# Sixteen small products ahead of TensorE's first work in a fused attention and gated MLP kernel

## The chip, the cores and the metric

The kernel runs on one core of a Trainium2 chip. The metric is the device time of one execution in microseconds; lower is better. Times of a kernel are medians over several runs.

## The reference

All inputs are float32. Chunked attention over 4 x 8 heads of 768 positions with 64 values each: a chunk of 32 queries sees 8 memory positions and a window of up to 56 positions around it. What it gives, 512 wide per position, goes through a gated MLP: a product with `w_in` and a rectifier, a split into u and v, a normalization of v, a product of v along the sequence with `w_spatial`, the gate, and a product with `w_out`.

```python
scores = scale * np.matmul(q_c, k_full.transpose(0, 1, 3, 2))
scores = scores - np.max(scores, axis=-1, keepdims=True)
a = np.exp(scores)
a = a / (np.sum(a, axis=-1, keepdims=True) + 1e-09)
out[:, :, c_start:c_end] = np.matmul(a, v_full)
...
h = np.maximum(x @ w_in, 0.0)
u, v = (h[..., :d_ff // 2], h[..., d_ff // 2:])
mu = np.mean(v, axis=-1, keepdims=True)
var = np.mean((v - mu) ** 2, axis=-1, keepdims=True)
v_n = (v - mu) / np.sqrt(var + 1e-06)
v_s = np.einsum('ts,bsd->btd', w_spatial, v_n) + b_spatial[None, :, None]
gated = u * v_s
return (gated @ w_out).astype(np.float32)
```

## The kernel before

Attention goes in 24 units of 128 queries (four chunks, all heads), six units to a batch element. A unit is one step of `attend`: `burst` (line 600) issues the scores of unit i, and the products of weights and values of unit i - 1, as short runs of small float32 products, 32 for each part. The profile shows two matmuls with a weight load each for one such product, so a part is 64 matmuls, 128 instructions; from unit 4 on both parts stand in one burst of 256 instructions. `softmax` (from line 700) has VectorE take the maximum and the difference (lines 713, 717) and ScalarE the exponential (line 732). `flip` turns p and the attention output: for the first nine units on TensorE (lines 788 and 815, tiles pt and xt), later on VectorE. Everything behind that is products in pairs of high and low parts (float32r), issued in `group` (line 872): three products for each pair of operands, from 384 to 512 columns wide. Weights are split into such pairs by `from_f64` (lines 1056 to 1084) as their loads land; `stage_w` and `stage_z` are the tiles for half of `w_in`.

All of this goes into a list of operations (`Plan`). `Plan.order` lays them out in time by given costs and writes one fixed order per engine; `ORDER` shifts single operations. The order of TensorE's instructions is therefore the same in each run, and each engine takes its own in that order. The planner also counts TensorE's instructions and lets a page of `PAGE` = 256 of them be fetched while the one before it runs (lines 205 to 210); that count begins at its first operation.

Ahead of the plan (lines 329 to 338) GpSimd writes `ident`, a unit matrix of 128 x 128, VectorE fills small constants, and ScalarE makes `minus` from `ident`. TensorE does nothing there. PSUM has eight banks' worth of tiles: four "f", and pools for "sx" (scores), "pt" and "xt".

Of the kernel before, what the change touches and what calls it, by code (L numbers as in the profile page):

```python
# [8 lines left out]
F32 = mybir.dt.float32  # L9
# [9 lines left out]
CH = 32  # L19
# [40 lines left out]
}  # L60
PAGE = 256
FETCH = 2.4
VLATE = 0
PSUB = 0
# [41 lines left out]
class Plan:  # L106
# [42 lines left out]
    def order(self):  # L149
# [19 lines left out]
        while len(out) < len(ops):  # L169
# [31 lines left out]
            if count:  # L201
# [3 lines left out]
                for m in range(begun, begun + count):  # L205
                    if m % PAGE == 0:
                        at = max(at, fetched.get(m // PAGE, 0.0))
                        fetched[m // PAGE + 1] = max(at, pipe) + FETCH
                    at += each
# [34 lines left out]
def tile_chunked_attention_gmlp(  # L244
# [22 lines left out]
    nc = tc.nc  # L267
    B, H, D, S = q.shape
# [4 lines left out]
    P = 128  # L273
# [29 lines left out]
    def pool(name, **kw):  # L303
        return ctx.enter_context(tc.tile_pool(name=name, **kw))
# [12 lines left out]
    ps = {name: pool(f"ps_{name}", bufs=sizes[name], space=PSUM) for name in ("f", "sx", "pt", "xt")}  # L317
# [7 lines left out]
    ident = const.tile([P, P], F32, name="ident")  # L325
# [3 lines left out]
    halves = const.tile([P, 2], F32, name="halves")  # L329
    warm = const.tile([P, 1], F32, name="warm")  # L330
    make_identity(nc, ident)
    nc.vector.memset(mhalf, -0.5)
    nc.vector.memset(tiny, 1e-9)
    for r in range(2):
# [1 line left out]
        nc.vector.memset(halves[r * D:(r + 1) * D, r:r + 1], 1.0)  # L336
    nc.scalar.activation(warm, mhalf, AF.Exp)
    nc.scalar.activation(minus, ident, AF.Copy, scale=-1.0)

    hot = [n for n in HOT]  # L340

# [875 lines left out]
```

## Time and profile before

| | |
|---|---|
| median of 3 runs | 383.62 us (383.19 to 385.25) |
| span of the profiled execution | 383.0 us |
| its TensorE matmuls | 358.4 us busy (94%) |
| ScalarE, VectorE, GpSimd | 253.2 (66%), 205.2 (54%), 152.3 us (40%) |

The span runs from the first to the last instruction of one profiled execution. A matmul row and its weight load are two instructions; sums over "PE" are matmuls alone, "PEld" the weight loads. "Idle before <- X" is time in which the engine did nothing and what ended it; "issue" means that the profile shows nothing that ended it. Semaphore instructions are not in these rows. Queue 8 and queue 14 carry instructions, queue 1 the loads and stores that SyncE issues; the share of a queue is the time of its packets over the time of 16 DMA engines in the stretch, put down to the stretch in which a packet starts (so it can be above the stretch itself).

### The profile page before, as it was taken

What the parts mean: (1) busy time and instruction counts of PE and PEld (TensorE: products, weight loads), DVE (VectorE), ACT (ScalarE), POOL (GpSimd) and SP (SyncE); (2) the same over time, 40 slices, a digit from 0 to 9 for tenths busy, and PEclk for the clock granted to TensorE, in tenths of its full rate; (3) what the DMA queues carried; (4) which work ended last, traced back from release to release, by engine and by line L of the source; (5) the groups of instructions that cost most, each with busy time, mean ns of one, the idle gap of its engine ahead of it and who ended that gap; (6) DMA issues with size and microseconds to landing.
All of it is one profiled execution on the core that took longest, in us unless ns stands there. A gap on an engine that the chain in (4) does not pass through costs nothing.

```text
span 383.0 us, 11256 instructions
## 1 busy us (share of the span) xinstructions
PE 358.4 (94%) x4692; PEld 321.0 (84%) x4692; DVE 205.2 (54%) x408; ACT 253.2 (66%) x659; POOL 152.3 (40%) x230
## 2 busy tenths in 40 slices
PE   1484999989999999999999999999999999999996
PEld 0353898989899889899899889899899889999995
DVE  1785877866436366665546274764555363613030
ACT  5873998863575968878876878879777883411212
POOL 5781887556424323325614423304514410213031
PEclk9998799999999999999999999999999999999999
DMA  7988926862123154124121433115120100000202
GB/s 225 319 272 183 317 84 154 288 192 82 34 86 105 72 146 98 50 75 146 48 86 55 170 90 107 50 49 171 51 86 2 55 29 2 1 0 3 82 0 84
DMA packets 29243, 39.71 MB, mean 104 GB/s; under 512 B 5192, under 2 KB 23304, under 8 KB 29192
## 3 DMA queue, kind: packets, MB, share of 16 engines
q1 hardware_dynamic: 28968, 38.91, 32.6%
q8 instruction: 37, 0.61, 0.7%
q14 instruction: 14, 0.11, 0.1%
q10 hardware_dynamic: 224, 0.08, 0.1%
HBM read 32.69 MB, written 6.29 MB: 102 GB/s over the span
## 4 chain that ended last, share of the span: by engine, by line
PE 81%; ACT 7%; DVE 4%; issue 3%; POOL 2%; DMA 1%; SPq 0%; ACTq 0%; POOLq 0%
PE f L872 70%; PE sx L602 8%; ACT xs L690 2%; POOL st L1058 2%; ACT pT L363 2%; PE pt L788 1%; DMA big<-in_moe_w_in_dram 1%; PE xt L815 1%; DVE mx L713 1%; ACT p L732 1%; PE f L602 1%; DVE p L717 1%; ACT big L991 1%; DVE vn L934 0%; ACT pT L791 0%
## 5 line engine op out<-in xcount | busy, mean ns | idle before, releaser
L872 PE MATMUL f<-wsp_h,vn 128*128 128x384 f32 x384 | 99.1, 339 | 0.0
L872 PE MATMUL f<-x,win_h 128*128 128x384 f32 x256 | 72.6, 341 | 0.0
L872 PEld LDWEIGHTS f<-wsp_h,vn 128*128 128x128 f32 x384 | 69.3, 188 | 2.6
L872 PE MATMUL f<-wout,big 128*128 128x512 f32 (+1 forms) x300 | 71.4, 382 | 0.0
L872 PE MATMUL f<-wsp_l,vn 128*128 128x384 f32 x192 | 64.5, 336 | 0.0
L690 ACT COPY xs<-sx 32x128 f32<-32x128 f32 x240 | 61.4, 256 | 3.5 <-PE sx L602 0.6
L872 PE MATMUL f<-win_h,x 128*128 128x512 f32 x192 | 62.9, 408 | 0.5 <-ACT x L821 0.2
L872 PEld LDWEIGHTS f<-wout,big 128*128 128x128 f32 x300 | 54.3, 188 | 9.1
L988 POOL TENSOR_TENSOR st<-st,u 128x384 f32<-128x384 f32 x32 | 33.4, 1044 | 66.9 <-DVE st L984 45.9
L872 PEld LDWEIGHTS f<-x,win_h 128*128 128x128 f32 x256 | 47.0, 188 | 1.4
L915 POOL TENSOR_TENSOR rstd<-ve,mhalf 128x1 f32<-128x1 f32 x24 | 15.3, 637 | 74.1 <-DVE ve L911 65.0
L363 ACT COPY pT<-p 32x128 f32<-32x128 f32 x144 | 42.6, 296 | 2.3 <-POOL p L768 0.5
L872 PE MATMUL f<-x,win_l 128*128 128x384 f32 x128 | 43.3, 338 | 0.0
L872 PEld LDWEIGHTS f<-win_h,x 128*128 128x128 f32 x192 | 35.2, 191 | 7.7 <-DVE x L825 0.5
L991 ACT CAST big<-st 128x384 fp32r<-128x384 f32 x32 | 16.4, 512 | 35.8 <-POOL st L988 35.4
L984 DVE TENSOR_TENSOR st<-f,bias 128x384 f32<-128x384 f32 x32 | 17.8, 556 | 39.4 <-PE f L872 39.0
L872 PE MATMUL f<-win_l,x 128*128 128x512 f32 x96 | 38.3, 399 | 0.3 <-DVE win_l L1084 0.3
L872 PEld LDWEIGHTS f<-wsp_l,vn 128*128 128x128 f32 x192 | 36.1, 188 | 0.0
L995 DVE TENSOR_TENSOR big<-st,big 128x384 fp32r<-128x384 f32 x32 | 19.4, 606 | 24.8 <-ACT big L991 24.8
L768 POOL TENSOR_TENSOR p<-p,rec 128x512 f32<-128x512 f32 x15 | 15.7, 1046 | 40.8 <-DVE rec L745 39.9
L363 POOL COPY pT<-p 32x128 f32<-32x128 f32 x96 | 29.9, 312 | 4.3
L602 PEld LDWEIGHTS sx<-k,q 64*32 64x32 f32 x1536 | 17.8, 112 | 14.2 <-POOL k L363 7.7
(91 smaller groups left out, 514.4 us busy)
## 6 DMA issues: line engine op xcount, KB each, us to landing
out_dram<-st SPq DMA_DIRECT2D x23, 256.0 KB
k<-in_k_dram SPq DMA_DIRECT2D x7, 800.0 KB
q<-in_q_dram SPq DMA_DIRECT2D x7, 768.0 KB
vmain<-in_v_dram SPq DMA_DIRECT2D x38, 128.0 KB
vmain<-in_v_dram SPq DMA_DIRECT2D x37, 96.0 KB
big<-in_moe_w_spatial_dram SPq DMA_DIRECT2D x6, 384.0 KB
big<-in_moe_w_in_dram SPq DMA_DIRECT2D x4, 512.0 KB
stage_w<-in_moe_w_in_dram SPq DMA_DIRECT2D x4, 512.0 KB
```

Source lines behind the costliest of these rows:

```text
L363: (nc.scalar.copy if e == "ACT" else nc.gpsimd.tensor_copy)(o, a)
L602: nc.tensor.matmul(o, w_, m, start=start, stop=True, skip_group_check=True)
L690: (nc.scalar.copy if e == "ACT" else nc.vector.tensor_copy)(o, a)
L713: nc.vector.tensor_reduce(mx, s, axis=AX.X, op=ALU.max)
L768: (nc.vector if e == "DVE" else nc.gpsimd).tensor_tensor(p3, p3, rec, op=ALU.mult)
L872: nc.tensor.matmul(o, ll if x == 1 else lh, rl if x == 2 else rh, start=x == j == 0, stop=j == len(pairs) - 1 and x == (single[-1] if sing ...
L915: nc.gpsimd.tensor_tensor(a, t_["ve", i], mhalf, op=ALU.pow)
L984: nc.vector.tensor_tensor(alloc("st", s_, [P, HT], F32), t_["f", n], bias[:, tok], op=ALU.add)
L988: nc.gpsimd.tensor_tensor(a, a, t_["u", i], op=ALU.mult)
L991: nc.scalar.copy(t_["g", i][:, 0, 0:HT], t_["st", s_])
L995: nc.vector.tensor_tensor(a[:, 1, 0:HT], t_["st", s_], a[:, 0, 0:HT].bitcast(F32), op=ALU.subtract)
L1058: nc.gpsimd.tensor_scalar(o, a, 2.0 ** -112, None, op0=ALU.mult)
```

## The change

Behind the constants, and ahead of the first operation of the plan, TensorE gets sixteen float32 products of `ident` with itself: 64 rows, 32 columns of weights, two moving columns each. They write two columns of a PSUM tile of tag "xt", which nothing reads. The plan, its order and all other instructions stay as they are. In TensorE's stream each instruction behind them stands 64 places further on.

```diff
--- before.py
+++ after.py
@@ -59,6 +59,7 @@
     319: (31, 0, ''), 320: (-34, 3, ''), 321: (-34, 1.5, ''), 323: (-32, 0.4, ''),
 }
 PAGE = 256
+PADS = 16
 FETCH = 2.4
 VLATE = 0
 PSUB = 0
@@ -329,6 +330,7 @@
     halves = const.tile([P, 2], F32, name="halves")
     warm = const.tile([P, 1], F32, name="warm")
     make_identity(nc, ident)
+    ps_pad = ps["xt"].tile([P, 512], F32, tag="xt", name="xt")
     nc.vector.memset(mhalf, -0.5)
     nc.vector.memset(tiny, 1e-9)
     for r in range(2):
@@ -336,6 +338,9 @@
         nc.vector.memset(halves[r * D:(r + 1) * D, r:r + 1], 1.0)
     nc.scalar.activation(warm, mhalf, AF.Exp)
     nc.scalar.activation(minus, ident, AF.Copy, scale=-1.0)
+
+    for _ in range(PADS):
+        nc.tensor.matmul(ps_pad[0:CH, 0:2], ident[0:D, 0:CH], ident[0:D, 0:2], start=True, stop=True)
 
     hot = [n for n in HOT]
```

## Rows read from the trace of the kernel before

**Rows 1.** The page: span, TensorE's busy time with instructions, and its instruction queue.

```profile
span 383.0 us, 11256 instructions
...
PE 358.4 (94%) x4692; PEld 321.0 (84%) x4692; DVE 205.2 (54%) x408; ACT 253.2 (66%) x659; POOL 152.3 (40%) x230
...
q8 instruction: 37, 0.61, 0.7%
```

**Rows 2.** Waits of TensorE: waiter, releaser: us in total, times, longest us.

```profile
PE f L602 <- issue: 5.3, 1, 5.3
...
PE xt L815 <- DVE xs L665: 1.1, 1, 1.1
```

**Rows 3.** Timeline, TensorE: start us, us, line, tile, shapes, count [idle before, releaser].

```profile
5.49 1.19 PE L602 MATMUL sx<-k,q 64*32 64x64 f32 x64 [5.49 <-POOL k L363]
...
22.58 0.86 PE L602 MATMUL f<-vmain,pT 64*32 64x64 f32 x64
...
26.13 0.50 PE L872 MATMUL f<-win_h,x 128*128 128x512 f32 x1 [0.24 <-ACT x L821]
...
31.87 0.78 PE L602 MATMUL f<-vmain,pT 64*32 64x64 f32 x49
37.93 0.46 PE L602 MATMUL f<-vmain,pT 64*32 64x64 f32 x15 [5.29 <-issue]
```

**Rows 4.** Stretches: us, then PE, PEld, DVE, ACT, POOL busy, clock, DMA, GB/s.

```profile
0.00:32.60 32.60, 17.83 (x474) 12.89 (x475) 18.57 (x40) 20.52 (x34) 20.14 (x27) 1.00 0.85 269
...
0.00:166.40 166.40, 145.15 (x2337) 126.21 (x2337) 104.11 (x212) 118.92 (x271) 88.30 (x114) 0.98 0.51 156
0.00:193.70 193.70, 172.45 (x2719) 151.51 (x2719) 120.17 (x239) 140.16 (x334) 100.34 (x138) 0.98 0.49 148
...
38.30:42.80 4.50, 4.50 (x107) 3.75 (x108) 3.38 (x5) 3.72 (x6) 3.73 (x3) 0.50 0.87 290
...
82.37:383.00 300.63, 297.31 (x3382) 270.35 (x3382) 148.78 (x293) 191.95 (x553) 98.49 (x175) 1.00 0.22 71
```

**Rows 5.** DMA queues (packets, MB, share) in 20.8:20.95, 21:35.25 and 35.25:35.45 us.

```profile
q8 instruction: 1, 0.02, 45.7%
...
q1 hardware_dynamic: 1691, 3.36, 87.0%
...
q8 instruction: 1, 0.02, 35.5%
```

**Rows 6.** Timeline, GpSimd, first 6 us.

```profile
1.06 0.29 POOL masks.py:199 TENSOR_SCALAR_AFFINE_SELECT ident<-ident 128x128 f32<-128x128 f32 x1
```

**Rows 7.** Timeline, SyncE's loads around 26 us.

```profile
25.75 0.81 SPq L385 DMA_DIRECT2D stage_w<-in_moe_w_in_dram  x2
```

**Rows 8.** Timeline, ScalarE, then VectorE, 33 to 37 us.

```profile
33.24 0.66 ACT L1056 ACTIVATE stage_z<-stage_w 128x512 f32<-128x512 f32 x1 [4.77 <-DMA stage_w<-in_moe_w_in_dram]
...
36.51 0.61 ACT L732 ACTIVATE p<-p 128x512 f32<-128x512 f32 x1
...
33.93 0.43 DVE L1066 TENSOR_SCALAR stage_z<-stage_z 128x512 uint32<-128x512 uint32 x1 [3.39 <-ACT stage_z L1056]
```

**Rows 9.** Timeline, TensorE, around two later bursts.

```profile
166.43 0.86 PE L602 MATMUL sx<-k,q 64*32 64x64 f32 x64
...
169.37 0.34 PE L872 MATMUL f<-x,win_l 128*128 128x384 f32 x1
...
193.72 0.86 PE L602 MATMUL sx<-k,q 64*32 64x64 f32 x64
...
196.31 0.33 PE L872 MATMUL f<-wsp_l,vn 128*128 128x384 f32 x1
```

**Rows 10.** DMA queues in 167.4:167.55, 193.2:194.9 and 194.9:195.05 us.

```profile
q8 instruction: 1, 0.02, 40.2%
...
q1 hardware_dynamic: 286, 0.52, 80.6%
...
q8 instruction: 1, 0.02, 44.8%
```

## The prediction

> **What bounds the kernel now.** I read the page first. TensorE is busy 94% of the 383.0 us, and 37 packets of queue 8 carry 0.61 MB of instructions for 9384 recorded matmuls and weight loads [rows 1]: 16.4 KB and some 254 of these per packet. With the semaphore instructions between them that is 256 instructions of 64 bytes, the size the kernel calls PAGE. So TensorE's stream is fetched in pages of 256, and 37 x 256 - 9384 = 88 instructions are semaphores, one per 107 others.
>
> Next the waits of TensorE. One wait has no releaser, 5.3 us before a matmul of line 602 [rows 2]. The timeline puts it inside a burst: 49 matmuls run from 31.87 us, nothing follows for 5.29 us, and the other 15 start at 37.93 [rows 3]. A burst needs nothing between its 49th and 50th matmul, so I take this as a page that was not there. Up to there 474 matmuls have run [rows 4], 948 matmul instructions, so the border lies just behind them and the other borders are 256 instructions apart from it. The DMA view agrees: queue 8 has no packet from 21.0 to 35.25 us, then one starts that takes 35.5% x 16 x 0.2 = 1.14 us [rows 5]. It ends by about 36.5, and TensorE goes on 1.47 us later. From the packet's start to the restart it is 2.6 us.
>
> From 82.37 us on TensorE is busy 297.31 of 300.63 us [rows 4]: any stall there goes straight to the end. Before it, TensorE also waits for the other engines; the last such wait is 1.1 us for VectorE's xs [rows 2].
>
> **The products themselves.** Sixteen float32 products are 64 instructions, 32 matmuls with their loads: a burst of 32 products is 64 matmuls [rows 3]. By the nearest row, the burst at 5.49 (64 matmuls in 1.19 us), they cost 0.6 us [rows 3]. They need ident, whose select on GpSimd starts at 1.06 and takes 0.29 us [rows 6], so they run at about 1.4 to 2.0. TensorE is idle until 5.49 and waits there for GpSimd's k [rows 3]; that wait hides them with 3.4 us to spare. Cost 0; if the cover were gone, 0.6 us. They write the bank of xt, which no other work uses so early, and put nothing on another queue. A gain is excluded for the products alone, since nothing waits for them.
>
> **The border that stalls.** Each border moves 64 instructions (32 matmuls) back. The one at the 50th matmul of the burst at 31.87 goes to its 18th. What it fetches is needed a page later; the page that was late is the one that begins at this border, and its request went out at the border before, one page earlier: 128 matmuls back from the stall, less a few semaphores, at the matmul of 26.13 [rows 3]. From there to the packet it is 9 us. At 25.75 SyncE had issued two loads of 512 KB [rows 7], and between 21.0 and 35.25 the load queue kept 87% of the engines' time [rows 5]: the fetch stood behind loads. Moved by 32 matmuls the request goes out inside the burst at 22.58, near 22.9 [rows 3], before those two loads are issued. The page is needed at 32.0, so its packet may start as late as 32.0 - 2.6 = 29.4, 6.5 us after the request. A fetch did get in at 20.8, in traffic as full as this [rows 5]; I expect this one by about 28, when the loads issued ahead of it are through (an estimate between 22.9 and 29.4), and the 5.29 us go.
>
> The Trainium skill says of a DMA engine's queues (DMA: Bandwidth & Descriptors, Queues, rings and completion order) that an engine takes turns between queue rows, packet by packet. By that rule no fetch would wait 9 us behind loads; the rows disagree, and I go by them.
>
> **What is late next.** Not much is won by it. The work behind the burst is the turning of p, and p is written by ScalarE's exponential at 36.51, which ends at 37.12 [rows 8]. Its chain has nothing of TensorE in it: ScalarE waited 4.77 us for a load of stage_w until 33.24, VectorE behind it until 33.93, with the maximum and difference of p queued behind that [rows 8]. So TensorE reaches the turning at 37.12 in place of about 37.93 + 0.40: a gain of 1.2 us, not 5.3. The moved fetch also takes 1.14 us of one DMA engine ahead of stage_w in place of behind it; where that engine is the last to land, the chain starts later by as much and 0.1 us is left. Above, the clock: it is 0.50 from 38.3 to 42.8, 4.50 us of work [rows 4]. TensorE had idled since 32.65; in the new order it idles from about 33.1 to 37.1, so I expect the lower level (1.2 GHz) again. Were it at 2.4 GHz, 2.25 us more would go, 3.4 us in all. Between 0.1 and 3.4 I take 0.7 us, near the row of p, and expect the chain to xs at 82.37 to follow, since its engines too are fed by TensorE in that stretch.
>
> **The borders that become tight.** Behind 82 us the bursts are 128 matmuls, 256 instructions: exactly a page, in 1.5 us. A border early in a burst asks for the page that is needed just behind the burst. To 166.40 us 2337 matmuls have run [rows 4]: (2337 - 474) x 2 = 3726 instructions behind the stall, with one semaphore per 107 some 3761; the 15th border behind the stall (3840) lies 79 instructions into the burst that starts at 166.43 [rows 9]. The fetch row confirms it: a packet starts in 167.4 to 167.55 [rows 10], 1.0 us into the burst. Moved by 64, the border lies 15 instructions in, and the next one 15 instructions (7.5 matmuls) behind the burst's end, reached at 169.2 [rows 9]. 64 instructions of the burst take 0.35 us, so the packet starts near 167.1, takes 40.2% x 16 x 0.15 = 0.97 us [rows 10], and with the 1.47 us of the stall the page is there at 169.6: a stall of 0.4 us. The burst at 193.72 is the same (2719 matmuls [rows 4], border 76 in, 12 after the move). Its fetch starts in 194.9 to 195.05, right behind output stores that fill 193.2 to 194.9 [rows 10]. An earlier request doesn't get past them: 194.95 + 1.08 + 1.47 = 197.5, needed at 196.3 [rows 9]: 1.2 us; without the stores 0.9. A third burst of this kind, at 221.7, comes out near zero by the same reckoning. Bounds: the 1.47 us rest on one stall. Were the page usable as soon as its packet ends, all these stalls would be 0; two or three more borders that come right ahead of a burst could add up to 1 us, so 0 to 2.6. I take 1.5.
>
> **The sum.** The span of 383.0 stands 0.6 below the median of 383.62, and I carry that over: 383.0 - 0.7 + 1.5 + 0.6 = 384.4.
>
> **Rivals.** (a) *The gain carries through and the new borders hold*: the early gain is 1.2 to 3.4 us and no page is late. For it: fetches already overlap all but one border; against it: three bursts of 1.5 us with a turnaround of at least 2 us. 383.6 - 2.3 = 381.3, range 380.2 to 382.4. (b) *The new borders cost more than the old one*: slower. Its place is the code right behind the bursts at 166, 194 and 222; it decides once packet start to restart exceeds the 2.5 us used there. With the one that needed 2.6 plus 1 us of queueing behind stores or loads, each of the three loses about 1 us more: 383.6 - 0.5 + 3.9 = 387.0, range 385.5 to 388. (c) *The idle is no page border*, or the moved request meets the same traffic: the 5.29 us stay, the late borders count or not: 383.6 to 385.1, say 384.0. The Trainium skill's rule (Runtime: NRT & Kernel Launch, Instruction fetch mechanics) that crossing a 16 KiB boundary is mostly hidden would make the whole change worth nothing, 383.6; the 5.29 us in mid-burst speak against it.
>
> **How the numbers follow.** Forecast 0.52; (a) 0.18; (b) 0.18; (c) 0.12. A 0.5% step is 1.9 us, about what a measurement of this kernel can tell from no change: below 381.7 it is faster, above 385.5 slower. Of (a) about two thirds are below 381.7; of (b) all, and a few per cent of the forecast, are above 385.5. Faster 0.13, same 0.66, slower 0.21. The forecast's own bounds are 383.6 - 1.2 + 0 = 382.4 to 383.6 - 0.1 + 2.6 = 386.1; the range of 382.0 to 386.3 leaves out most of (a) and half of (b).
>
> **What would show it.** Right: no idle with no releaser at 32 to 38 us, TensorE waiting instead for ScalarE's p at about 37.1, a queue 8 packet between 23 and 28, and short idles with no releaser some 2.7 us behind the starts of the bursts near 166 and 194. Wrong: the turning of p much earlier than 37, which means that its chain isn't bound by stage_w; the clock at full level in 38 to 43; or a queue 8 packet that still waits for 35. If the late bursts show no idle, the 1.47 us of the one stall were not the fetch's own and the time falls to about 382.9.

## The result, and the profile after

The changed kernel took 387.99 us (median of 15 runs, 384.78 to 389.79), the kernel before, run beside it, 384.38. The ratio is 1.0083, with an interval of 1.0059 to 1.0108: slower by about 0.8%. The forecast was 384.4 in a range of 382.0 to 386.3; the time lies above it, in the range of rival (b), but not for that rival's reason. Two later measurements of the same code gave 1.0102 (1.0049 to 1.0155) and 1.0056 (1.0026 to 1.0085). A ratio leaves out runs that took over 1.5% more than the fastest run of the same kernel.

The profiled execution of the changed kernel took 389.5 us. The page shows TensorE as busy as before [rows 1] in a span 4.3 us longer:

```profile
span 387.3 us, 11320 instructions
...
PE 363.5 (94%) x4724; PEld 325.0 (84%) x4724; DVE 204.1 (53%) x408; ACT 253.8 (66%) x659; POOL 150.5 (39%) x230
...
q8 instruction: 37, 0.61, 0.7%
```

TensorE's waits with no releaser and its wait for xs, from the view of waits (waiter, releaser: us in total, times, longest):

```profile
PE sx L607 <- issue: 3.8, 2, 2.6
PE xt L820 <- DVE xs L670: 2.6, 2, 2.3
PE f L607 <- issue: 2.6, 1, 2.6
```

Where there was one wait with no releaser, of 5.3 us [rows 2], there are three. The timeline of TensorE places them (the first line is that of the sixteen products):

```profile
1.41 1.86 PE L343 MATMUL xt<-ident 64*32 64x2 f32 x32 [1.41 <-POOL ident masks.py:199]
...
19.10 0.43 PE L607 MATMUL sx<-k,q 64*32 64x64 f32 x7 [2.62 <-issue]
...
28.10 0.64 PE L607 MATMUL f<-vmain,pT 64*32 64x64 f32 x20 [2.58 <-issue]
...
37.66 1.02 PE L607 MATMUL f<-vmain,pT 64*32 64x64 f32 x64
39.39 0.66 PE L793 MATMUL pt<-ident,p 128*128 128x128 f32 x4 [0.71 <-ACT p L737]
...
41.51 0.86 PE L607 MATMUL sx<-k,q 64*32 64x64 f32 x64
...
59.80 0.21 PE L607 MATMUL sx<-v,pT 64*32 64x64 f32 x1 [1.16 <-issue]
...
85.21 1.08 PE L820 MATMUL xt<-ident,xs 128*128 128x128 f32 x4 [2.27 <-DVE xs L670]
```

The burst that had the old stall now runs whole, at 37.66, and TensorE waits for p behind it. Two stalls stand ahead of it, at the two borders that the prediction had not priced, and one stands ahead of the last matmul of unit 6's burst. All four borders, the old stall's among them, are whole pages apart: 252, 254 and 1016 recorded matmuls and weight loads, and 256, 256 and 1024 instructions with the semaphore instructions that the trace also holds. The page reading holds in every profile of this document: of 50 idle times of TensorE of 0.4 us and more that have no releaser, 48 end at the same place of a page.

Instruction by instruction against the profile of before, the 4.3 us add up so. At 28 to 34 us TensorE is some 6 us late, but at 57.6 only 0.35. What makes up for the two early stalls is that profile's own delay: its stall of 5.29 us stands there and not here, and its clock was low from 38.3 to 42.8. So this sum says little of what the early stalls cost; two more profiles of the kernel before, further on, start unit 4's burst near 38.8 us, and the changed kernel is some 2.7 us later there (41.51). The stall at 59.80 adds 1.36, the wait for xs 1.13, and then the clock adds 1.60: the same matmuls, from the turning of xs on, take 3.46 us here (85.21 to 88.67) and 1.86 in the kernel before. Behind that the distance stays at 4.3. Clock by stretch (us, busy times, clock, DMA, GB/s):

```profile
34.00:85.10 51.10, 46.54 (x961) 39.43 (x959) 39.44 (x80) 40.71 (x72) 32.92 (x28) 1.00 0.64 188
85.21:88.62 3.41, 3.41 (x13) 3.31 (x14) 2.58 (x5) 1.22 (x2) 2.11 (x3) 0.50 0.99 300
38.30:42.80 4.50, 3.60 (x139) 2.63 (x126) 3.80 (x10) 4.00 (x6) 3.06 (x4) 1.00 1.04 375
```

The lower level (1.2 GHz), which the kernel before had at 38.3 to 42.8 [rows 4], comes here at 85.21, behind the 2.27 us in which TensorE waited for xs.

The later xs has its own chain. SyncE's issues, then the engines that wait, in the changed kernel:

```profile
55.63 6.25 SPq L390 DMA_DIRECT2D vmain<-in_mem_v_dram  x8
...
66.97 3.28 SPq L390 DMA_DIRECT2D big<-in_moe_w_out_dram  x3
...
74.04 1.54 POOL L1063 TENSOR_SCALAR st<-big 128x512 f32<-128x512 f32 x1 [4.15 <-DMA big<-in_moe_w_out_dram]
...
76.15 0.60 DVE L928 SCALAR_TENSOR_TENSOR shift<-mvar,rstd 128x1 f32<-128x1 f32 x1 [1.71 <-POOL rstd L920]
```

In the kernel before the first two start at 55.18 (lasting 4.06 us) and 64.87, GpSimd's work at 71.03 and VectorE's at 73.35. So w_out is issued 2.1 us later, lands 3.0 us later, GpSimd stands at it, the rstd queued behind it comes late, and VectorE has xs in its queue behind that.

The late bursts show nothing. The burst of [rows 9] that stood at 166.43 stands at 170.70:

```profile
170.70 0.86 PE L607 MATMUL sx<-k,q 64*32 64x64 f32 x64
171.36 0.96 PE L607 MATMUL sx<-vmain,p 64*32 64x64 f32 x64
172.25 0.44 PE L877 MATMUL f<-x,win_h 128*128 128x384 f32 x1
```

No idle time stands behind it. Queue 8, in 170.1 to 170.3:

```profile
q8 instruction: 1, 0.02, 38.1%
```

Its packet starts at 170.2, ahead of the burst, not some 0.7 us inside it as reckoned.

### The profile page after: what moved, and what is told of

Same layout as the page of the kernel before. It is cut to its first block, busy times and chain, and to the rows that moved or that the text cites. A ratio compares the mean times of both kernels' runs of the same rounds, so it can differ in the third digit from the quotient of the medians.

```text
span 387.3 us, 11320 instructions
## 1 busy us (share of the span) xinstructions
PE 363.5 (94%) x4724; PEld 325.0 (84%) x4724; DVE 204.1 (53%) x408; ACT 253.8 (66%) x659; POOL 150.5 (39%) x230
## 4 chain that ended last, share of the span: by engine, by line
PE 77%; DVE 8%; ACT 7%; issue 4%; POOL 2%; DMA 1%; SPq 0%; ACTq 0%; POOLq 0%
PE f L877 67%; PE sx L607 7%; ACT xs L695 2%; ACT pT L368 2%; DVE mx L718 1%; DMA big<-in_moe_w_in_dram 1%; PE pt L793 1%; DVE p L722 1%; POOL st L1063 1%; DVE vn L939 1%; PE xt L820 1%; PE f L607 1%; ACT p L737 1%; DVE stage_z L1071 1%; ACT pT L796 1%
## 5 line engine op out<-in xcount | busy, mean ns | idle before, releaser
L996 ACT CAST big<-st 128x384 fp32r<-128x384 f32 x32 | 16.4, 512 | 35.7 <-POOL st L993 35.4
## 6 DMA issues: line engine op xcount, KB each, us to landing
big<-in_moe_w_spatial_dram SPq DMA_DIRECT2D x6, 384.0 KB
```

What stands on the lines that cost most here:

```text
L996: nc.scalar.copy(t_["g", i][:, 0, 0:HT], t_["st", s_])
```

## The experiments

Five theories were held, one after the other. **Theory 1**: the loss begins at the border next to unit 6's burst (the stall at 59.80, then xs, then the clock). **Theory 2**: it comes from the two early stalls. **Theory 3**: an instruction packet that starts inside the last load of w_spatial delays SyncE's next loads. **Theory 4**: the profiled execution of the kernel before was itself a late one. **Theory 5**: the early borders and those behind 38 us each give a part.

The table has every profiled execution, "profile" from here on. Borders are counted through TensorE's stream (for e2_page, which has a page more, through that of the kernel before). "2" to "5" are idle times (us) ahead of the first instruction behind them, between 16 and 46 us; "unit 6" is that at the borders from 50 to 61 us, "later" behind 100 us. The median is that of the runs made with the profile (for the kernel before, of all its 128 runs), the ratio that to the kernel before run beside them.

| profile | products | 2 | 3 | 4 | 5 | unit 6 | later | span | median | ratio |
|---|---|---|---|---|---|---|---|---|---|---|
| before | none | 0 | 0 | 5.29 | 0 | 0 | 0 | 383.0 | 384.3 | |
| r2_before | none | 1.03 | 0 | 0 | 0 | 0 | 0 | 381.2 | | |
| r3_before | none | 0 | 0 | 2.69 | 0 | 0 | 0 | 380.1 | | |
| e2_page | 16 front, 48 behind unit 0's scores | 0 | 0 | 2.96 | 0 | 0 | 0 | 382.1 | 384.56 | 1.0029 |
| e7_late12 | 12 at unit 5 | 0 | 0 | 2.96 | 1.09 | 0 | 1.38 | 383.5 | 385.77 | 1.0052 |
| e3_late16 | 16 at unit 5 | 0 | 0 | 0 | 0 | 0.43 | 0 | 382.8 | 385.68 | 1.0065 |
| e6_late20 | 20 at unit 5 | 0 | 0 | 3.02 | 0.70 | 1.60 | 1.60 | 385.9 | 388.02 | 1.0087 |
| e9_later | 16 at unit 3's p | 0 | 0 | 3.23 | 0 | 0 | 1.36 | 387.2 | 386.32 | 1.0053 |
| e12_later | the same | 0 | 0 | 2.68 | 0 | 0 | 0 | 381.3 | 385.16 | 1.0016 |
| after | 16 front | 2.62 | 2.58 | 0 | 0 | 1.16 | 0 | 387.3 | 387.99 | 1.0083 |
| r1_after | the same | 3.18 | 1.20 | 1.98 | 2.80 | 0 | 0 | 386.2 | 388.23 | 1.0102 |
| e11_after | the same | 2.89 | 0.66 | 1.99 | 1.43 | 0.18 | 0 | 383.3 | 387.25 | 1.0056 |
| e4_warm | 16 front, 8 wide at 81 us | 2.36 | 0.65 | 1.98 | 1.15 | 0.74 | 1.60 | 386.4 | 388.22 | 1.0123 |
| e5_both16 | 16 front, 16 at unit 5 | 2.61 | 2.58 | 0 | 0 | 0.74, 0.59 | 0 | 385.6 | 387.6 | 1.0087 |
| e8_early | 16 front, 48 at unit 3's p | 2.91 | 0.93 | 2.25 | 2.87 | 0 | 0 | 388.0 | 390.71 | 1.0201 |
| e10_early2 | 16 front, 24 and 24 at 38 and 46 us | 2.91 | 1.21 | 3.08 | 1.75 | 0 | 0 | 388.2 | 387.96 | 1.0087 |
| e1_pads12 | 12 front | 2.46 | 0 | 0 | 0 | 0 | 0 | 382.0 | 385.32 | 1.0043 |
| e15_pads24 | 24 front | 0 | 0 | 0 | 0 | 0 | 0.58 | 382.1 | 385.04 | 1.0019 |
| e13_pads32 | 32 front | 0 | 0 | 0 | 0 | 0.61 | 0 | 382.7 | 383.87 | 0.9988 |
| e14_pads32 | the same | 0 | 0 | 0 | 0 | 0.74 | 0 | 383.6 | 383.4 | 1.0002 |

**Twelve products, and a whole page of them.**

```diff
-PADS = 16
+PADS = 12
```

> Twelve products in front in place of sixteen: every border lies 16 instructions (8 matmuls) later than in the changed kernel, so the two early borders stay inside the same bursts, but the border that lay 2 instructions ahead of the burst of unit 6 now lies 14 instructions into it, and the next one 14 behind its end. Theory 1 (the loss starts at that border, near 58.6 us): a packet that again starts near 57.3 us is usable near 59.8, when it is needed too; no idle there or at most 0.3 us, the wait for xs near 83 us is about 1.1 us as in the kernel before, no fall of the clock behind it, median 384 to 385.5. Theory 2 (the loss comes from the two early stalls of 2.6 us each at 16.5 and 25.5 us): the same stalls, 2 to 3 us each, median 387 to 388.5.

```diff
+                    if i == 0:
+                        for _ in range(48):
+                            mm(ps_pad[0:CH, 0:2], ident[0:D, 0:CH], ident[0:D, 0:2])
```

> The sixteen products in front, and 48 more behind the scores of unit 0, where TensorE is idle from 6.9 to 12.3 us: 256 instructions in all, a whole page, so that from unit 1 on every border lies at the place that it has in the kernel before. Theory 1: no idle near 58.6 us, the wait for xs near 83 us as before, median 384 to 385.5. Theory 2: the page with unit 1's work is asked for near 7 us and needed near 14.4, its packet starts near 16 again: an early stall of 2 to 4 us, median 387 or more.

Measured: 385.32 (interval of the ratio 1.0012 to 1.0074), in theory 1's band, with the stall at the second border and none at the third; and 384.56 (1.0006 to 1.0052), where the early stall that theory 2 wanted did not come. With a whole page added the stalls are those of the kernel before, with 64 products run, and the loss is a third of the changed kernel's; what that third is, no run shows. So the place of the borders costs, and the products at most little.

**Later borders alone, and a TensorE kept busy.** The first has no products in front and puts sixteen at the head of unit 5's burst; the second is the changed kernel with eight wide products in the wait for xs.

```diff
-PADS = 16
+PADS = 0
...
+                    if i == 5:
+                        for _ in range(16):
+                            mm(sx[0:CH, 0, w_, 0, 0:2], ident[0:D, 0:CH], ident[0:D, 0:2])
```

> No products in front; sixteen at the head of unit 5's burst (near 49.6 us), into scores that the burst then overwrites. Borders up to there are as in the kernel before, those behind it as in the changed kernel. The products cost 0.6 to 0.9 us of busy TensorE. Theory 1: an idle of 1.0 to 1.5 us at the last matmul of unit 6's burst, the early one of 5.3 us at 32.7 is there as well, median 387 to 389. Theory 2: no loss beyond the products, 384.5 to 385.5.

```diff
+                if j == 7:
+                    for _ in range(8):
+                        nc.tensor.matmul(a.rearrange("p t q -> p (t q)"), minus,
+                                         minus.unsqueeze(1).broadcast_to([P, T, P]), start=True, stop=True,
+                                         skip_group_check=True)
```

> The changed kernel with eight wide products (512 columns, 0.23 us each at 2.4 GHz, 1.9 us in all) into the bank of xt ahead of the turning that waits for xs near 83 to 85 us; they run within the wait of 2.3 us. Theory of the clock (1.6 us of the loss are matmuls at the lower clock from 85.2 to 88.6, because TensorE stood idle): no fall of the clock there, 1.0 to 1.6 us less than the changed kernel, median 386.4 to 387. Rival (the lower clock costs nothing, the other engines set the pace there): 388, unchanged.

Measured: 385.68, between what the two theories gave, with a stall of 0.43 us where theory 1 wanted 1.0 or more; some 1 us of it are the products, which run from 48.23 to 49.20 us with nothing to hide them. The clock run has a mean clock of 1.000 in all but one of its six runs and still takes 388.22: the clock is not what the loss stands on. Its profile gives another reason, behind the burst near 222 us:

```profile
223.31 0.86 PE L607 MATMUL sx<-k,q 64*32 64x64 f32 x64
223.97 1.01 PE L607 MATMUL sx<-vmain,p 64*32 64x64 f32 x64
226.58 0.73 PE L882 MATMUL f<-win_h,x 128*128 128x512 f32 x2 [1.60 <-issue]
```

The eight products (16 instructions) moved one border from 17 instructions inside this burst to its start and the next from 15 behind it to its very end, and that one costs 1.60 us. This is the stall that the prediction looked for behind the late bursts.

**The border at unit 6's burst, moved by itself.** Sixteen more at unit 5 behind sixteen in front; then twenty and twelve there with none in front.

```diff
 PADS = 16
+                    if i == 5:
+                        for _ in range(16):
```

> The changed kernel with sixteen more of the small products at the head of unit 5's burst, so that the border 2 instructions ahead of unit 6's burst lies 66 ahead of it, and its packet is requested before the last load of w_spatial is under way. The two early stalls stay as they are. They cost about 1 us of TensorE at 48 us. Theory 3 (an instruction packet that starts inside the last load of w_spatial holds that load up by 2 us, SyncE's next loads wait for it, and through w_out, GpSimd and VectorE the xs at 83 us): the eighth load of mem_v is issued within 4.6 us of that of w_spatial instead of 6.3, xs is there by 83.5 instead of 85.2, time 385 to 386.5 against 388 of the changed kernel. Theory 2 (the loss comes from the two early stalls): they are still there, so 388 to 389, with the 1 us of products on top or not.

```diff
-                        for _ in range(16):
+                        for _ in range(20):
```

> No products in front, twenty at the head of unit 5's burst: the early borders are those of the kernel before, and the border at unit 6's burst lies 18 ahead of it instead of 2 as in the run with sixteen there. Theory 3: the packet is requested some 0.5 to 1 us earlier, so it starts inside the load of w_spatial in most executions, the next loads go out 6 us behind it instead of 4, and the time is 387 to 388. Theory 1 (the stall inside unit 6's burst itself): the border is not right ahead of the burst any more, the stall is at most 0.3 us, time 385 to 385.7, no more than with sixteen. Theory 2: no early stall, 384.5 to 385.5.

```diff
-                        for _ in range(16):
+                        for _ in range(12):
```

> No products in front, twelve at the head of unit 5's burst: the border lies 14 instructions inside unit 6's burst. Theory 3: requested a little later than with sixteen, the packet starts behind the load of w_spatial, time 384.5 to 385.5. Theory 1: the next border is 14 instructions behind the burst, a stall of 0.5 to 1.2 us there, and the time is 385.5 to 387. Theory 2: 384.5 to 385.5.

> The changed kernel again, for a second look at the same code and for its times beside the other three on one chip. Theory 3: if in this execution the packet at unit 6's burst starts inside the load of w_spatial, the load that follows goes out 6 us behind it and the span is 386 to 387.6; if it starts ahead of the load or behind it, 4 to 4.6 us and a span of 382.5 to 384.5. Theory 2: the span follows the two early stalls, and not the place of that packet. Median 387 to 388.5.

e7_late12, at 385.77, fits theory 1 by time, but its profile has no stall at unit 6's burst; what it has is 1.09 us at the fifth border, 1.38 us near 282 and 0.7 us of products. Theory 3's mechanism shows in the traces: in the four profiles where a packet began 0.9 to 2.1 us behind the issue of w_spatial's last load (after, e4_warm, e11_after, e13_pads32) SyncE issued the eighth load behind it 5.3 to 6.4 us after that issue, in the sixteen others 4.0 to 4.8 us. But it does not set the time. r1_after has 4.1 us there and a span of 386.2, e11_after 5.6 us and 383.3, and moving the border off (e5_both16) left the time where it was. e6_late20 came out at 388.02 as theory 3 wanted, but its profile shows 4.7 us, and TensorE's own stalls instead: 1.60 us at unit 6's burst and, as in e4_warm, right behind the burst near 222:

```profile
226.07 0.73 PE L880 MATMUL f<-win_h,x 128*128 128x512 f32 x2 [1.60 <-issue]
```

The second profile of the changed kernel (r1_after) showed the pattern that five of the seven with sixteen in front have, four late pages in a row:

```profile
19.84 0.44 PE L607 MATMUL sx<-k,q 64*32 64x64 f32 x7 [3.18 <-issue]
...
27.46 0.64 PE L607 MATMUL f<-vmain,pT 64*32 64x64 f32 x20 [1.20 <-issue]
...
38.81 0.74 PE L607 MATMUL f<-vmain,pT 64*32 64x64 f32 x47 [1.98 <-issue]
...
45.09 1.14 PE L607 MATMUL sx<-v,pT 64*32 64x64 f32 x59 [2.80 <-issue]
```

The queues from 37.40 to 42.75 and in 42.75 to 42.95, in the same profile:

```profile
q1 hardware_dynamic: 1129, 1.77, 94.9%
...
q8 instruction: 1, 0.02, 32.1%
```

TensorE gets over the fourth border at 38.81, and the page behind the fifth can be asked for only then; its packet starts near 42.8, behind loads that keep 95% of the DMA engines' time, and the burst has needed it since 42.3. A late page makes the next request late. The 2.80 us go to the end whole: against the first profile of the kernel before TensorE is 0.3 us early at the start of unit 4's burst, 2.5 us late behind it, and 3.3 at the end.

**The kernel before again, and the two halves.** Two further profiles of the kernel before, unchanged; then 48 products ahead of the turning of unit 3's p, behind sixteen in front, and sixteen there with none in front.

> The kernel before, a second look. Theory 4 (the profiled execution of the kernel before was late in its early part, and the 5.29 us that the prediction priced were not usual): four runs with the same early borders showed 3.0 us or none at that border, and unit 4's burst 1.4 to 2.4 us earlier than the profile of before. So here: a stall of at most 3.2 us inside the burst at 32 us, unit 4's burst at 39.1 to 40.2 us instead of 41.5, a span of 381 to 382. Rival: the old profile was usual; a stall over 4.5 us, the burst at 41 to 42, a span near 383.

> The kernel before, a third look; as for the second. If the border of unit 4's burst, which held in the first profile, is as much a matter of the execution as theory 4 has it, one of the two looks may show a stall of 0.7 to 1.1 us inside that burst, as two of the runs with the same border did.

```diff
+                for k in range(48 if i == 3 else 0):
+                    c, r = k % 2 * 2 + k // 2 % 2, k % 2
+                    nc.tensor.matmul(a[c * CH:(c + 1) * CH, r, 0:2], ident[r * D:(r + 1) * D, 0:CH],
+                                     ident[r * D:(r + 1) * D, 0:2], start=True, stop=True, skip_group_check=True)
```

> The sixteen products in front as in the changed kernel, and 48 more ahead of the turning of unit 3's p, where TensorE waits for p anyway (0.7 us in the changed kernel; they run for 1 to 1.5 us, so up to 0.8 us may show): the borders up to 38 us are those of the changed kernel, all behind them those of the kernel before. Theory 2 (early stalls make all of it): 387 to 388.5. Theory 5 (both parts add up: the early stalls some 1.2 us, the borders behind 38 us the rest): 385 to 386.2. If the early part costs nothing: 384 to 384.8.

```diff
-PADS = 16
+PADS = 0
...
+                for k in range(16 if i == 3 else 0):
```

> No products in front, sixteen ahead of the turning of unit 3's p, hidden in its wait: the borders up to 37 us are those of the kernel before, all behind them those of the changed kernel. Theory 5: 385.8 to 387, with stalls inside unit 4's or unit 6's burst that TensorE carries to the end. Theory 2: 384 to 384.8. If the borders behind 38 us make all of it: 387.5 to 388.5.

Theory 4 held: the spans are 381.2 and 380.1 us, and unit 4's burst came even a little ahead of what was expected. The third profile of the kernel before (second fence: the second):

```profile
32.12 0.78 PE L602 MATMUL f<-vmain,pT 64*32 64x64 f32 x49
35.59 0.34 PE L602 MATMUL f<-vmain,pT 64*32 64x64 f32 x15 [2.69 <-issue]
35.87 0.93 PE L788 MATMUL pt<-ident,p 128*128 128x128 f32 x4
...
38.86 1.06 PE L602 MATMUL sx<-k,q 64*32 64x64 f32 x64
```

```profile
36.67 0.66 PE L788 MATMUL pt<-ident,p 128*128 128x128 f32 x4 [1.17 <-ACT p L732]
...
38.71 0.86 PE L602 MATMUL sx<-k,q 64*32 64x64 f32 x64
```

One has 2.69 us at that border and one nothing but a wait for p, and both start unit 4's burst near 38.8, not at 41.5. In these two the stall is hidden in that wait: with or without it the burst comes at the same time. Over all nine profiles with these early borders it was 5.29 once, 2.7 to 3.2 six times and nothing twice. It also gives a measure of what the early stalls cost: in these nine, unit 4's burst starts between 38.7 and 42.0 us, in the middle at 40.1; in the five with sixteen in front and nothing else added ahead of it, between 39.9 and 41.5, in the middle at 41.2. Some 1 us of the early stalls is left there, and the stall at the fifth border, which three of these five have, comes on top.

e8_early says little: its 48 products ran into a border of their own and stood 2.87 us there. e9_later gave 386.32 (1.0018 to 1.0088), in theory 5's band, but its profile has no stall at unit 4's or unit 6's burst, where theory 5 wanted one; it has 1.36 us near 286 and the lower clock behind xs.

**The halves once more, and half a page.** The first has 24 products ahead of the turning of unit 3's p and 24 ahead of the turning of an xs.

```diff
+                for k in range(24 if i == 3 else 0):
...
+                for k in range(24 if j == 3 else 0):
...
```

> Sixteen products in front, 24 ahead of the turning of unit 3's p and 24 ahead of the turning of the xs near 46 us, each some 0.5 us, in places where TensorE waits 0.3 to 0.7 us: the borders up to 38 us are those of the changed kernel, the one at unit 4's burst lies about 31 instructions inside it, all behind 47 us are those of the kernel before. Theory 5 (the parts add up, early 1.0 to 1.5 us): 385.2 to 386 with the kernel before at 384.3. Theory 2 (early stalls make all of it): 387.5 to 388.5. If the early part costs nothing: 384 to 384.8.

> The changed kernel on the same chip and in the same rounds as the two halves: 387.5 to 388.3. Its span follows the stalls behind 38 us: each at unit 4's or unit 6's burst goes to the end whole, and where there is none the span is 382.5 to 384.

> The later half again (sixteen products ahead of the turning of unit 3's p). Theory 5: 1.5 to 2.5 us over the kernel before, and with the early half's 1.0 to 1.5 the changed kernel's 3 to 4. Theory 2: within 0.5 us of the kernel before.

```diff
-PADS = 16
+PADS = 32
```

> Thirty-two products in front: 128 instructions, half a page. They take some 3.7 us from 1.4 us on, still ahead of k at 5.4. The early borders come 64 instructions earlier in the work than in the changed kernel; unit 4's and unit 6's bursts have them near the bounds of the work ahead of them and the middle of their second half. If the place of the borders sets the time: the bursts of unit 4 and 6 have no border within 20 instructions of either end, no stall over 0.3 us there, and 384 to 385.8. If each further product or each move of the early borders costs: 388 or more.

> Thirty-two products in front again: 383.5 to 384.8, within 0.3% of the kernel before; no stall at the second and third border (near 17 and 25 us), and at most one of about 0.6 us in unit 6's burst. If the first run was a chance: 385.5 or more.

```diff
-PADS = 16
+PADS = 24
```

> Twenty-four products in front: 96 instructions. The second border lies 32 instructions earlier in the work than in the changed kernel, in the turning of xs and the scores near 15 to 16 us, so its page is needed about 1 us earlier than there, while the packet comes at 16 to 17.5 us as in all runs: a stall of 2 to 4 us at that border, and 386 to 389. If the loss depends on something else than when a page is needed and when its packet comes: no stall there, 384 to 385.

The later half alone gave 385.16 here (0.9996 to 1.0037), below theory 5's 1.5 to 2.5 us over the kernel before, and 385.40 over its 22 runs; the changed kernel gave 387.25, and 387.5 over its 31 runs. So of some 3.2 us over the kernel before, the later borders make about 1.1 and, by subtraction, the early ones about 2.1 (by means in place of medians 1.6 and 1.5). The early half alone (e10_early2) came out at 387.96 (1.0056 to 1.0118), above theory 5's 386 and in the band of theory 2: its fifth border, 1.75 us, and up to 1 us of products are its own, so it bounds the early part from above only, and that the early part makes all of the loss is not excluded by it:

```profile
39.16 0.68 PE L607 MATMUL f<-vmain,pT 64*32 64x64 f32 x44 [3.08 <-issue]
...
45.63 0.67 PE L607 MATMUL sx<-k,q 64*32 64x64 f32 x42 [1.75 <-issue]
```

e11_after has 1.43 us at the fifth border and still a span of 383.3, where its expectation came to 383.9 or more.

Twice the products cost nothing that shows: 383.87 (0.9958 to 1.0017) and 383.4 (0.9969 to 1.0034), though one late page of 0.6 or 0.7 us stands near 52 to 58 us, where the first of the two expectations wanted none. The tile of tag "xt" is taken there as in the changed kernel, so it is not what costs either. With 24 my expectation missed by sign: no stall at the second border, and no loss that shows (0.9984 to 1.0054, runs from 382.34 to 389.07). I had reckoned with the packet at 16 to 17.5 us. With 32 products a packet starts near 7.4 (queue 8 in 7.3 to 7.5; the other two fences are the changed kernel in 6.5 to 16.2, where queue 8 has no packet, and in 16.2 to 17):

```profile
q8 instruction: 1, 0.02, 29.6%
```

```profile
q1 hardware_dynamic: 2094, 2.78, 90.6%
```

```profile
q8 instruction: 1, 0.02, 9.8%
```

With 24, with 32 and with the whole page the first packet after the start comes at 6.9 to 7.9 us, and the second border never waits. In the eight others with 16 or 12 in front it comes at 16.3 to 17.2, and TensorE stands at the second border for 2.4 to 3.2 us, every time. Nothing beat the kernel before by more than its interval.

## Why the prediction was wrong, step by step

- **The products cost nothing**: right, by the cover and not by the price. They take 1.86 us (1.41 to 3.27) where 0.6 were reckoned, and the wait for k still has 2.4 us to spare. The first burst starts at 5.67 in place of 5.49 in the first profile, and between 5.38 and 5.56 in the others with sixteen in front.
- **The border that stalls**: the 5.29 us went in the first profile, but not for the reason given, and in five of the seven with sixteen in front 1.98 to 3.08 us stand there again. The packet was to start by 28. It starts at 35.5, as in the kernel before [rows 5]; the one at 25.8 serves the border ahead of it. Queue 8 in 25.7 to 25.9 and in 35.4 to 35.6:

```profile
q8 instruction: 1, 0.02, 29.2%
...
q8 instruction: 1, 0.02, 35.7%
```

The request was to go out near 22.9, at the third border; TensorE, held up twice, got over that border only at 28.1. It then came to the fourth at 37.8 and not at 32.65, so no wait is left. The step itself was sound where nothing held TensorE up ahead of it: with 12, 24 and 32 products in front it is over the third border at 22.6 to 25.0, the packet starts 1.0 to 2.5 us later, and none of the four profiles has a stall at the fourth border (with 24 it lies at the start of the burst below). Where it got over that border at 26.0 to 29.3, the packet started 6.0 to 10.2 us later in 14 of 16 profiles.

```profile
34.67 0.94 PE L607 MATMUL f<-vmain,pT 64*32 64x64 f32 x64
```

- **A gain of 0.7 us**: this step sized a stall by one execution. Over nine profiles it was mostly 2.7 to 3.2, and in the one that was followed further the wait for p took it up. That wait was named in "What is late next", rightly, but at 37.9 to 38.3 of an execution that was some 2.7 us late there. There was no 5 us to win.
- **Other borders**: this is the main failed step. The sum priced the one border that stalled and those behind 82 us, and put the rest at nothing. The second and third, which the change moved as well, had no row because they had no stall. They cost 2.4 to 3.2 and 0.65 to 2.6 us each time. Part of that is hidden by the wait for p, and some 1 us is left at the start of unit 4's burst; where the fifth border follows late, its 1.15 to 2.8 us come on top, behind any wait that could hide them.
- **"Before 82 TensorE also waits for the other engines"**: taken as cover, which it is up to the wait for p at 39 and no further. The stalls in unit 4's and unit 6's bursts went on: 2.80 in r1_after and 1.16 in the first profile whole, where they were followed to the end.
- **Tight borders behind bursts**: priced 1.5, measured 0 in all three profiles of the changed kernel. The borders lie where the step put them. But it took a border to be crossed when its instruction runs; at the first two of these bursts the packet starts 0.5 and 1.9 us ahead of the burst (170.2 and 196.1 in the first profile), so the request leaves before. At the third it starts 1.0 us inside, and that one had been reckoned near zero. The rest of the step was sound: with the borders sixteen instructions earlier in the work (e4_warm, e6_late20) the stall at the third is 1.60 us both times, and TensorE goes on 1.35 and 1.57 us behind the end of the packet, where 1.47 were reckoned. Over the 48 stalls it is 1.26 to 1.67 us, and 2.00 once.
- **The 0.6 us between span and median**: mis-sized. Every later run lies 2.2 to 2.4 us above its span, so the span of 383.0 belongs to the run of 385.25, 1.6 us above the median of 383.62. The kernel before itself is 384.3 over its 128 runs, so 0.7 us of the miss is the number that the sum started from.
- **The clock** was expected low at 38 to 43 and was not; it fell at 85 in the first profile, alone of the seven with sixteen in front. It is a part of that profile's 4.3 us, not of the loss: r1_after and e11_after have no such fall, nor has e4_warm.
- **Rival (b)** had the amount, 387.0, and a late page as its cause; its place, behind the bursts at 166, 194 and 222, was wrong, so that its number came out is luck.

What stays open in part is why the first packet comes at 7 us with 24 or 32 products and at 16 with 16. With 16 the border lies two instructions ahead of the end of unit 0's scores, behind which TensorE waits for p until 12.3. Either the request was out at 6.8 and waited 9.5 us, or it went out only at 12.3. One profile bears on it: e2_page has the same sixteen in front and this border at the same place, but 48 products follow it at once:

```profile
6.37 2.80 PE L607 MATMUL xt<-ident 64*32 64x2 f32 x50
```

The DMA engines are as busy from 6.5 to 8.0 us (0.84 of the time, 0.82 in the changed kernel), and the packet starts at 7.86. So with 16 the request most likely left only when TensorE went on at 12.3, and the page that was needed at 16.5 was asked for some 4 us ahead; with 24 it was asked for near 6 and needed at 15.9. This rests on one profile, and no view shows a request. Nor is the division of the loss exact, since the two halves were not both clean.

## What to carry to other kernels

When an edit shifts an instruction stream, list every page border in the part that is short of DMA, with the time at which its page can be asked for and the time at which it is needed; a border with no stall in the profile can get one. A stall seen in one execution is worth what the next engine's wait leaves of it, and a second profile of the same code says what it usually is. If a stream must be shifted, try a half and a whole page of filler beside the shift wanted: here these told that the position was at fault and not the products.

## What was not expected of the hardware

- Late pages come in series: in five of the seven profiles with sixteen products in front, four borders running stalled, 0.65 to 3.2 us each. After each of the 48 stalls the next packet started behind the restart, by 1.0 us or more, and from 37.40 to 42.75 us of r1_after no instruction packet got through. The Trainium skill (Runtime: NRT & Kernel Launch, Instruction fetch mechanics) says that the next page is fetched while the current one runs and that the cost is mostly hidden. The rows agree for over 30 of the 37 packets of each profile; where they disagree, it is mostly ahead of 46 us, where the DMA engines are busy about 90% of the time.
- Where one instruction packet started inside a load, 0.9 to 2.1 us behind its issue, SyncE's eighth load behind it came 1 to 2 us later than elsewhere (four profiles against sixteen), though the packet itself takes about 1 us of one engine.
- One program spreads over 6 us (384.0 to 390.2 over the changed kernel's 31 runs), and its profiles differ in which borders stall.
- A wait of about 2 us for xs was followed by the lower clock level in two profiles (2.27 us in the changed kernel, 1.98 in e9_later, mean 0.57 from 83.80 to 87.30) and not in a third (1.97 in e1_pads12, 1.00 from 81.52 to 85.00).
